# Second MoE layer by seven half-size products per 512-token block, with whole-batch q/k loads and 4-byte block transposes, in a fused attention and MoE kernel

## The chip, the cores and the metric

The kernel runs on one core of a Trainium2 chip. The metric is the device time of one execution in microseconds (us), on the slowest core, which here is the only core. A "ratio" below is the mean time of one kernel's fast runs over the mean of the other's fast runs of the same rounds, so it is not quite the ratio of the medians that are quoted beside it. Executions over 1.5% slower than the fastest of the same kernel are left out of the means.

Engines in the profile: PE is TensorE, PEld its weight loads, DVE is VectorE, ACT is ScalarE, POOL is GpSimd. L194 is line 194 of the kernel that the line comes from, so the numbers differ between kernels.

## The reference

Eight batches of eight heads, 576 tokens of 64 numbers each, are attended in chunks of 64 tokens. The result is laid out as x with 4608 tokens of 512 numbers, and passes through two matrix layers with a swish between them.

```python
# q, k, v: [8, 8, 576, 64];  w_in [512, 2048];  w_out [2048, 512];  beta [2048]
scores = scale * q_c @ k_c^T                # per chunk of 64 tokens
attn   = softmax(scores)
x      = (attn @ v_c).transpose(0, 2, 1, 3).reshape(4608, 512)
h      = x @ w_in
g      = h * (1 / (1 + exp(-beta * h)))
out    = g @ w_out                          # [4608, 512]
```

The kernels compute the sigmoid by a tanh: ScalarE makes `sg = tanh(beta/2 * h)`, VectorE makes `gt = (sg + 1) * h`, and the output is scaled by 0.5.

## The kernel before

Work is cut into blocks of 512 tokens (the first two of 256). For a block, sixteen groups `m` of four matmuls make the first layer. Each group fills one PSUM buffer `hps`; ScalarE reads it, then VectorE reads it and so frees it. The second layer makes four output tiles of sixteen matmuls each. Both layers share four PSUM buffers (pool `ps_p`).

```python
ps_p = tile_pool(name="ps_p", bufs=4, space=PSUM)

def emit_m(j, m):                           # first layer, one group
    hps = ps_p.tile([128, n], FP32, tag="p", name="hps")
    for kk in range(KDM):                   # 4 matmuls 128x512
        nc.tensor.matmul(out=hps, lhsT=w_in16[...], rhs=xt_t[j][:, kk, :], ...)
    nc.scalar.activation(out=sg, in_=hps, func=Tanh, scale=...)
    nc.vector.scalar_tensor_tensor(out=gt_t[j][:, m, :], in0=sg, scalar=1.0, in1=hps,
                                   op0=ALU.add, op1=ALU.mult)     # frees hps

def emit_t(j, t):                           # second layer, one tile of 128 tokens
    ops = ps_p.tile([128, DM], FP32, tag="p", name="ops")
    for kk in range(KFF):                   # 16 matmuls 128x512
        nc.tensor.matmul(out=ops, lhsT=gt_t[j][:, kk, ...], rhs=w_out16[:, kk, :], ...)
    nc.scalar.activation(out=osb, in_=ops, func=Copy, scale=0.5)  # frees ops

def emit_T(u):                              # q and k of 256 tokens; 2-byte elements,
    ...                                     # output step of 2 elements = 4 bytes
    nc.vector.transpose(out=t[:, :, :, :, r], in_=a[:, :, r, :]...)
# [...] loads, scores, values and the order of emission are cut here
```

In steady state the order is: groups m = 0 to 3 of block j, then the second layer of block j-1 with the attention of the next block between its tiles, then groups 4 to 15 of block j. VectorE's instructions appear in the traces in the order of emission: in the timeline after, below, an evacuation whose input is ready at 165.59 us starts at 171.06 us, behind four transposes that were emitted before it.

The softmax here doesn't subtract the row's maximum and nothing guards it: scores larger than these inputs give would overflow.

## Time and profile before

| | before |
|---|---|
| time, median of 4 runs | 347.41 us (346.66 to 349.46) |
| span of the profiled run | 348.3 us |
| TensorE busy | 288.9 us (83%) |
| VectorE busy | 175.7 us (50%) |
| start of the first first-layer matmul | 40.98 us |
| one block in steady state | 30.80 us |

The page of the kernel before: total busy times, then the busy share of TensorE in 40 slices (in tenths), then the share of each engine in the chain of work that ended last.

```profile
PE 288.9 (83%) x2944; PEld 142.9 (41%) x2944; DVE 175.7 (50%) x305; ACT 144.5 (41%) x234; POOL 77.2 (22%) x100
...
PE   0110274983998599999999999999999999999995
...
PE 77%; DMA 14%; DVE 3%; issue 2%; POOL 2%; ACT 1%; ACTq 0%; DVEq 0%; POOLq 0%
```

TensorE starves in the first third of the slices, which is a matter of loading (its longest wait, of 21.3 us, is for a transposed tile, while DMA is at nine tenths), and then is full to the end. The chain says the same: 77% of it is TensorE.

The chain of the kernel before, one block in steady state. Columns: start, duration, what.

```profile
200.69 13.81 PE hps L181 x64
214.87 3.56 PE ops L197 x16
219.44 3.56 PE ops L197 x16
223.37 3.56 PE ops L197 x16
227.93 3.56 PE ops L197 x16
231.49 13.81 PE hps L181 x64
```

One block lasts 231.49 - 200.69 = 30.80 us: 64 matmuls of each layer, 13.81 us for 64 (216 ns apart), and some 3 us of attention between the tiles. TensorE waits for nobody here, so a shorter second layer would shorten the block directly, if TensorE still waits for nobody afterwards.

Two neighbouring lines of its timeline, in the first layer. The bracket at the end of a line is the idle time of that engine before it, and what ended it.

```profile
205.04 0.69 ACT L189 ACTIVATE sg<-hps,beta_sb 128x512 f32<-128x512 f32 x1 [0.17 <-PE hps L181]
205.76 0.69 DVE L190 SCALAR_TENSOR_TENSOR gt<-sg,hps 128x512 f16<-128x512 f32 x1 [0.17 <-ACT sg L189]
```

VectorE spends 0.69 us of every 0.86 us on evacuations while the first layer runs. In that stretch it has 0.17 us to spare per group, although over the whole span it is busy only half the time.

### The profile page before, as it was taken

The numbers are of one execution on the slowest core, as the hardware profiler recorded it, in microseconds if no ns is written. First come the engines' busy times: TensorE is split into PE (matmuls) and PEld (weight loads), VectorE is DVE, ScalarE is ACT, GpSimd is POOL, SyncE is SP. The second block draws the span as 40 slices with busy tenths as digits, with TensorE's granted clock in tenths as the row PEclk, the third lists the DMA queues.
The fourth block names the chain that finished last, engine by engine and source line by source line (L and its number), as shares of the span: only waits on it lengthen the run. The fifth ranks groups of instructions, "written<-read, shape, count | busy, mean of one in ns | idle before, by whom it ended". The sixth has DMA issues, their size and how long they took to land.

```text
span 348.3 us, 7008 instructions
## 1 busy us (share of the span) xinstructions
PE 288.9 (83%) x2944; PEld 142.9 (41%) x2944; DVE 175.7 (50%) x305; ACT 144.5 (41%) x234; POOL 77.2 (22%) x100
## 2 busy tenths in 40 slices
PE   0110274983998599999999999999999999999995
PEld 0110263561443245445544444444444444444442
DVE  1413083662649264685377468637745822720700
ACT  1110153361357222752573275257427623732711
POOL 8628286803053035005402100000000000000000
PEclk9999997896799899999999999999999999999999
DMA  9999999999095949909952900420131042002011
GB/s 97 186 178 186 194 158 169 173 181 147 15 150 52 88 78 180 107 10 122 189 48 51 192 31 2 108 77 0 49 98 39 2 98 86 2 30 86 6 60 60
DMA packets 106223, 32.97 MB, mean 95 GB/s; under 512 B 97488, under 2 KB 101584, under 8 KB 106192
## 3 DMA queue, kind: packets, MB, share of 16 engines
q0 software_dynamic: 79360, 18.36, 61.9%
q1 hardware_dynamic: 26832, 14.17, 17.8%
q8 instruction: 23, 0.38, 0.5%
q14 instruction: 8, 0.07, 0.1%
HBM read 36.71 MB, written 9.44 MB: 132 GB/s over the span
## 4 chain that ended last, share of the span: by engine, by line
PE 77%; DMA 14%; DVE 3%; issue 2%; POOL 2%; ACT 1%; ACTq 0%; DVEq 0%; POOLq 0%
PE ops L197 37%; PE hps L181 34%; DMA ku<-in_k_dram 6%; PE x L156 3%; DMA xt_99<-x_362 2%; DMA xt_101<-x_865 2%; DMA xt_100<-x_548 2%; DMA xt_102<-x_1414 2%; DVE qT L122 1%; DVE kT L122 1%; DVE gt L190 1%; POOL qu L87 1%; POOL vbig L95 1%; ACT sg L189 0%; POOL ku L87 0%
## 5 line engine op out<-in xcount | busy, mean ns | idle before, releaser
L190 DVE SCALAR_TENSOR_TENSOR gt<-sg,hps 128x512 f16<-128x512 f32 (+1 forms) x160 | 100.5, 634 | 99.4 <-ACT sg L189 99.1
L189 ACT ACTIVATE sg<-hps,beta_sb 128x512 f32<-128x512 f32 (+1 forms) x160 | 102.4, 645 | 72.8 <-PE hps L181 68.1
L197 PE MATMUL ops<-w_out_97,gt 128*128 128x512 f16 x576 | 129.9, 380 | 0.0
L181 PEld LDWEIGHTS <-w_in_96 128*128 128x128 f16 x640 | 64.7, 102 | 107.0 <-issue 42.4
L197 PEld LDWEIGHTS <-gt 128*128 128x128 f16 x576 | 54.1, 98 | 62.9 <-issue 0.5
L205 ACT ACTIVATE osb<-ops 128x512 f32<-128x512 f32 x36 | 21.5, 597 | 109.9 <-PE ops L197 95.5
L87 POOL DMA_DIRECT2D qu<-in_q_dram x24 | 19.0, 795 | 98.9 <-DVE qT L122 55.7
L95 POOL DMA_DIRECT2D vbig<-in_v_dram x40 | 33.9, 862 | 8.3 <-DMA w_in_96<-in_moe_w_in_dram 5.2
L122 DVE STREAM_TRANSPOSE kT<-ku 128x512 f16<-128x512 f16 x36 | 24.2, 722 | 21.7 <-DMA ku<-in_k_dram 21.7
L181 PE MATMUL hps<-xt_99,w_in_96 128*128 128x256 f16 x64 | 10.0, 323 | 23.1 <-DMA xt_99<-x_362 21.3
L122 DVE STREAM_TRANSPOSE qT<-qu 128x512 f16<-128x512 f16 x36 | 23.4, 699 | 0.0
L162 DVE RECIPROCAL rd<-x 128x8 f32<-128x8 f32 x36 | 7.2, 199 | 32.1 <-PE x L156 32.1
L181 PE MATMUL hps<-xt_101,w_in_96 128*128 128x512 f16 x64 | 17.4, 431 | 5.9 <-issue 5.1
L137 PEld LDWEIGHTS <-kT 32*64 32x64 f16 x1152 | 11.5, 111 | 22.0 <-DVE kT L122 9.1
L87 POOL DMA_DIRECT2D ku<-in_k_dram x24 | 18.9, 789 | 5.8 <-DMA w_out_97<-in_moe_w_out_dram 4.5
L181 PE MATMUL hps<-xt_102,w_in_96 128*128 128x512 f16 x64 | 15.8, 411 | 3.9 <-DMA xt_102<-x_1414 3.9
L181 PE MATMUL hps<-xt_100,w_in_96 128*128 128x256 f16 x64 | 9.5, 309 | 6.2 <-DMA xt_100<-x_548 4.4
L181 PE MATMUL hps<-xt_103,w_in_96 128*128 128x512 f16 x64 | 14.1, 379 | 0.0
L181 PE MATMUL hps<-xt_104,w_in_96 128*128 128x512 f16 x64 | 14.1, 379 | 0.0
L181 PE MATMUL hps<-xt_105,w_in_96 128*128 128x512 f16 x64 | 14.1, 379 | 0.0
L181 PE MATMUL hps<-xt_106,w_in_96 128*128 128x512 f16 x64 | 14.1, 379 | 0.0
L181 PE MATMUL hps<-xt_107,w_in_96 128*128 128x512 f16 x64 | 14.1, 379 | 0.0
(190 smaller groups left out, 124.4 us busy)
## 6 DMA issues: line engine op xcount, KB each, us to landing
out_dram<-osb SPq DMA_DIRECT2D x36, 256.0 KB, 2.0
vbig<-in_v_dram POOLq DMA_DIRECT2D x32, 128.0 KB, 7.4
qu<-in_q_dram POOLq DMA_DIRECT2D x12, 256.0 KB, 6.6
ku<-in_k_dram POOLq DMA_DIRECT2D x12, 256.0 KB, 8.2
w_in_96<-in_moe_w_in_dram POOLq DMA_DIRECT2D x4, 512.0 KB, 12.2
w_out_97<-in_moe_w_out_dram POOLq DMA_DIRECT2D x4, 512.0 KB, 8.8
qu<-in_q_dram POOLq DMA_DIRECT2D x4, 192.0 KB, 4.1
ku<-in_k_dram POOLq DMA_DIRECT2D x4, 192.0 KB, 7.6
```

Source lines behind the costliest of these rows:

```text
L87: nc.gpsimd.dma_start(out=t[off // 2:(off + n) // 2], in_=src[b, :, s:s + n, :].rearrange("h (p r) d -> p h r d", r=2),)
L95: nc.gpsimd.dma_start(out=vbig[off:off + n, i, :, 0:D], in_=v[b, :, s:s + n, :].rearrange("h p d -> p h d"),)
L122: nc.vector.transpose(out=t[:, :, :, :, r], in_=a[:, :, r, :].rearrange("p h (e i) -> p h e i", e=2),)
L137: nc.tensor.matmul(out=sc[c // 2][o0:o0 + 64, h, :], lhsT=kt[p0:p0 + 32, h, e].rearrange("p i r -> p (i r)"), rhs=qt[p0:p0 + 32, h, e].rea ...
L156: nc.tensor.matmul(out=x[p0:p0 + 64, h // 4, h % 4, 0:D + 1], lhsT=et[p0:p0 + 64, h, :], rhs=vbig[p0:p0 + 64, i, h, 0:D + 1],)
L162: nc.vector.reciprocal(out=rd, in_=x[:, :, :, D:D + 1])
L181: nc.tensor.matmul(out=hps, lhsT=w_in16[:, kk, m * 128:(m + 1) * 128], rhs=xt_t[j][:, kk, :], start=(kk == 0), stop=(kk == KDM - 1),)
L189: nc.scalar.activation(out=sg, in_=hps, func=ACTF.Tanh, scale=beta2_sb[:, m:m + 1])
L190: nc.vector.scalar_tensor_tensor(out=gt_t[j][:, m, :], in0=sg, scalar=1.0, in1=hps, op0=ALU.add, op1=ALU.mult)
L197: nc.tensor.matmul(out=ops, lhsT=gt_t[j][:, kk, t * 128:(t + 1) * 128], rhs=w_out16[:, kk, :], start=(kk == 0), stop=(kk == KFF - 1),)
L205: nc.scalar.activation(out=osb, in_=ops, func=ACTF.Copy, scale=0.5)
```

## The change

The intent is to do less work on TensorE, the engine that bounds the kernel. For a 512-token block the second layer is a product of two matrices, each cut into 2x2 parts. Strassen's scheme (here in Winograd's form) makes it with seven products of half size instead of eight. Seven products are 112 matmuls of 128x256 where 64 of 128x512 were before. The scheme pays with additions: four sums of parts of `gt` for each block, four of `w_out` once, and sums of products at the end. At the same time q and k are loaded for a whole batch in runs of 18 tokens where it was 2, are transposed in blocks as 4-byte words, and the heads sit on four row quadrants of 32 partitions. Block 0 keeps a plain second layer; block 1's attention is emitted after it, with transposes on TensorE.

The diff, cut to its core:

```diff
 def emit_T:
-    nc.vector.transpose(out=t[:, :, :, :, r], in_=...)              # 128x512, 2-byte
+    nc.vector.transpose(                                            # 128x576, 4-byte
+        out=dst[b][:, h2]....bitcast(FP32).rearrange("p (t r) -> p r t", r=RUN),   # RUN = 18
+        in_=src[b][:, h2]....bitcast(FP32).rearrange("p (r d) -> p r d", r=RUN))
+
+def emit_sums(j, a, n):                      # VectorE, 4 ops of 128x1024 fp16
+    tt(out=s1[:, lo], in0=g[:, lo, dn], in1=g[:, hi, dn], op=ALU.add)
+    tt(out=s2[:, lo], in0=s1[:, lo], in1=g[:, lo, up], op=ALU.subtract)
+    tt(out=s3[:, lo], in0=g[:, lo, up], in1=g[:, lo, dn], op=ALU.subtract)
+    tt(out=s4[:, lo], in0=g[:, hi, up], in1=s2[:, lo], op=ALU.subtract)
+
+def steps_L2(j):                             # seven products of 16 matmuls 128x256
+    st0: A  = g11*b11;  ScalarE u1 = A/2     # four PSUM buffers: A, B, D, C
+    st1: B  = g12*b21;  VectorE out11 = B/2 + u1
+    st2: A += s2*t2;    ScalarE u2
+    st3: D  = g22*t4
+    st4: A += s3*t3;    ScalarE u3;  VectorE out21 = D/2 + u3;  GpSimd w1 = u2 - u3
+    st5: C  = s4*b22
+    st6: A += s1*t1;    ScalarE o22 = A/2;  GpSimd w2 = w1 + o22;  VectorE out12 = C/2 + w2
 [...]
 for j in range(1, NB):
     for m in range(KFF):
-        if m == 4: ... emit_t(j - 1, t) with attention steps between
+        if m == 4 and j >= 2:
+            for n, st in enumerate(steps_L2(j - 1)):
+                st()
+                if at and n < 6:
+                    at.pop(0)()              # one attention step
+            if j + 2 < B:
+                for h2 in range(2):
+                    emit_T(j + 2, h2)        # four transposes
         emit_m(j, m)
+        if m in (11, 15):
+            emit_sums(j, m - 11, 4)
```

The products `st0` to `st6` are written as formulas here; in the kernel each is sixteen matmul calls and the named operations.

## The prediction

> **What bounds it now.** The page's engine table has TensorE busy 83%. The chain of waits shows two phases. Up to about 85 us TensorE starves: the first first-layer matmul starts at 40.98 us, after a 21.3 us wait for a transposed tile, and DMA is at nine tenths in the slices. From 139 us TensorE never waits: successive 512-token blocks are 30.80 us apart (169.89, 200.69, 231.49): 64 first-layer and 64 second-layer 128x512 matmuls (13.81 us each, 216 ns apart) plus about 3.1 us of attention. In the first layer each 0.69 us VectorE evacuation is followed by 0.17 us idle.

> **Removed.** Strassen makes 112 matmuls of 256 columns out of 64 of 512 in the second layer. The timeline shows 256-column matmuls with a weight load each at a pace of 109 ns (20 in 2.35 us), so 12.2 us replaces 13.8: 1.6 us per block, for 8 of 9 blocks: 13 us. Eight transposes of 512 per block become about four of 576.

> **Added, on VectorE, which is in order.** Per block: eight fp16 sums of 128x1024. [...] Also three output combinations (0.69 us each, as the same op is today); the third waits for a ScalarE copy (0.60) and then a GpSimd add[...].

> **On the critical path.** Only four PSUM buffers serve both layers. An evacuation frees its buffer about 1.75 us after its matmuls; the other three cover 2.6 us, so slack is about 0.9 us. Four sums[...] come after m=11 and m=15: about 2 us of TensorE stall each, the second when product A wants a buffer. After product seven the third combination holds VectorE about 2 us waiting for GpSimd, [...]: another 3 us in blocks with transposes. Walking the instruction order with these durations, a block takes about 35.5 us (29.1 of TensorE work plus 6.5 stalled) where transposes are, 33.5 without, against 30.8 now. So the saved 1.6 us turns into a loss of 3 to 5 us per block.

> **Start.** PE transposes replace DMA transposes in blocks 0 and 1[...]. First layer of block 0 starts near 27 us (now 41); its plain second layer ends near 59; block 1's attention is then emitted serially, TensorE mostly idle about 18 us; block 1's first layer starts near 77. This gains about 11 us on the present start.

> **Sum:** 77 + 21 + 4x35.8 + 2x33.8 + 30 + 12.2 + 4: about 355; with cold-clock matmuls, 357 us. Range 343 to 372. Chances: faster by over 2% 0.10, within 2% 0.32, slower by over 2% 0.58.

> **What would show it.** Right: second-layer matmuls 109 ns apart; TensorE idle of about 2 us before product A and around m=8 and the next m=0, released by VectorE evacuations; VectorE busy over 65%; blocks 33 to 37 us apart; a TensorE hole of 15 to 20 us near 60 us. Wrong: block distance near 29.5 us (sums hidden), or first-layer starts before 20 us.

> **What would make it wrong.** [...] 4-byte block transposes at half rate: about +9 us. Sums much faster than thought, or the hole at 60 us small: below 343.

The sum came to 355 us, and to 357 with 2 us for the low clock. Where the text shows a cut there stood a duration, or a claim about packets, that no trace or run of this case had shown: what a sum, a GpSimd addition and a transpose cost, when the first batch lands, and a risk of slower sums. The terms of the waits were worked out with these durations. So the waits of 2 and 3 us, the blocks of 35.5 and 33.5 us (35.8 and 33.8 in the sum), the 9 us of the other risk and the share of VectorE are estimates that no trace had shown. The 1.75 us of an evacuation is an estimate too; in the trace before, 1.61 us lie between the start of a group's last matmul (201.39) and the end of its evacuation (203.00). "Cold-clock matmuls" are matmuls at a lower granted clock, which that trace has: the clock is 0.50 from 85.09 to 90.00 us, and 16 matmuls from 85.09 us on take 6.40 us, where 16 at 216 ns would be 3.5 us.

## The result

| | before | after |
|---|---|---|
| time, median of 4 runs | 347.41 us (346.66 to 349.46) | 376.0 us (375.01 to 376.22) |
| ratio, 95% interval | | 1.080 (1.076 to 1.084) |
| span of the profiled run | 348.3 us | 373.1 us |
| mean granted TensorE clock | 0.968 | 0.939 |

The changed kernel is correct and 8% slower. The prediction had 357 us, with a range up to 372; the direction was right and the size was not.

The same lines of the page after:

```profile
PE 290.0 (78%) x3296; PEld 173.5 (47%) x3296; DVE 220.1 (59%) x354; ACT 140.0 (38%) x216; POOL 83.8 (22%) x82
...
PE   0149995479589867995889588958899699889893
...
PE 48%; DVE 32%; issue 8%; ACT 4%; DMA 4%; POOL 3%; POOLq 0%; DVEq 0%
```

TensorE's slices no longer stay at nine. Its busy time did not fall at all, although it has less to compute; matmuls on a slowed clock count as longer (at a clock of 0.50, 5 or 6 of 128x512 begin in 1.70 us, at 1.00 it is 9; see the windows below). VectorE, which was 3% of the chain, is now 32% of it.

Who waits for whom, after. Columns: engine, what waits, for what; us in total, times, longest.

```profile
DVE osb L275 <- POOL w L314: 26.3, 8, 4.3
PE hps L194 <- DVE gt L205: 23.8, 10, 3.9
...
PE oA L257 <- DVE gt L205: 10.4, 8, 1.4
```

TensorE loses 34 us to evacuations by VectorE, where the first layer lost 4.4 us to them before. VectorE in turn waits 26 us for the last GpSimd addition of each block.

The next lines are one block of the timeline after, in the order of time. `osb<-oC,w` is the last combination of the second layer, the four STREAM_TRANSPOSE are q and k for two blocks ahead, `gt<-sg,hps` are the evacuations that free first-layer buffers, L219 to L222 are the sums.

```profile
164.81 1.27 POOL L314 TENSOR_TENSOR w<-w,o 128x512 f32<-128x512 f32 x1 [3.19 <-issue]
...
166.12 0.69 DVE L275 SCALAR_TENSOR_TENSOR osb<-oC,w 128x512 f32<-128x512 f32 x1 [2.98 <-POOL w L314]
...
166.73 1.25 DVE L118 STREAM_TRANSPOSE qT<-qu 128x576 f32<-128x576 f32 x1
...
167.82 1.24 DVE L118 STREAM_TRANSPOSE kT<-ku 128x576 f32<-128x576 f32 x1
...
168.90 1.23 DVE L118 STREAM_TRANSPOSE qT<-qu 128x576 f32<-128x576 f32 x1
169.98 1.24 DVE L118 STREAM_TRANSPOSE kT<-ku 128x576 f32<-128x576 f32 x1
171.06 2.46 DVE L205 SCALAR_TENSOR_TENSOR gt<-sg,hps 128x512 f16<-128x512 f32 x4
171.79 9.80 PE L194 MATMUL hps<-xt,w_in 128*128 128x512 f16 x32 [3.90 <-DVE gt L205]
...
179.69 0.69 DVE L219 TENSOR_TENSOR s<-gt 128x1024 f16<-128x1024 f16 x1
...
182.96 3.61 PE L194 MATMUL hps<-xt,w_in 128*128 128x512 f16 x16 [1.37 <-DVE gt L205]
...
188.00 1.91 PE L257 MATMUL oA<-w_out,gt 128*128 128x256 f16 x16 [1.43 <-DVE gt L205]
```

Read it as one story. VectorE stands idle for 2.98 us because its next instruction waits for GpSimd (whose addition takes 1.27 us of that and itself comes after TensorE's last product and a copy by ScalarE). Then it does four transposes, one every 1.08 us, together 4.3 us (166.73 to 171.06). Only then come the evacuations. Meanwhile TensorE has filled all four buffers and waits 3.90 us. The 32 matmuls after that wait take 9.80 us, although 32 at 216 ns would be 6.9 us. The other two waits of a block, before the first group of the next block (182.96) and before product A (188.00), are 1.4 us each; both come behind four sums in a row. In the two blocks without transposes VectorE's wait for GpSimd is there too, and TensorE then waits only 0.27 us: it takes the transposes behind that wait to make the long one.

Why the 32 matmuls were slow is seen in windows around the wait. Columns: window, its length, TensorE busy time with the number of matmuls, granted clock; the last two columns, for DMA, are not used here.

```profile
164.00:167.90 3.90, 3.61 (x16) 1.00 0.48 107
...
171.80:173.50 1.70, 1.70 (x5) 0.50 0.98 140
173.50:175.20 1.70, 1.70 (x6) 0.50 1.05 202
175.20:176.90 1.70, 1.70 (x6) 0.50 1.20 186
...
178.60:180.30 1.70, 1.70 (x9) 1.00 2.45 157
```

After the wait the clock is 0.50 for about 5 us. In windows of 0.1 us the clock goes to 0.50 between 2.6 and 4.1 us after TensorE's last matmul, in all four blocks. The way back took 2.7, 5.6, 3.6 and 2.7 us of matmuls. So the wait is paid twice, once as a wait and once as slow matmuls.

The last table of the profile after: the stretches from one block's first group to that of the next, for blocks 1 to 7, then the last block's up to near its end. Columns: window, length, busy time of PE, PEld, DVE, ACT and POOL with the number of instructions, granted clock, and two for DMA.

```profile
78.20:103.76 25.56, 19.95 (x257) 8.36 (x257) 21.42 (x34) 12.92 (x20) 5.07 (x6) 0.83 1.30 103
103.76:143.40 39.64, 33.59 (x368) 19.65 (x369) 26.53 (x40) 14.87 (x23) 7.58 (x8) 0.89 0.76 83
...
221.43:259.50 38.07, 30.96 (x368) 19.05 (x368) 24.88 (x40) 15.56 (x24) 2.53 (x2) 0.96 0.16 44
259.50:292.20 32.70, 29.50 (x368) 18.75 (x368) 20.64 (x36) 15.56 (x24) 2.54 (x2) 1.00 0.18 50
```

There are two kinds of block. Four blocks with transposes last 38.1 to 39.6 us; two without last 32.7 and 32.8 us at full clock. Both are longer than the 30.80 us of before. From one product A to the next the distances are 38.1, 39.5, 38.5 and 38.1 us with transposes and 32.7 us without. The excess of 5.4, 6.8, 5.8 and 5.4 us is accounted for in each block: a wait of 3.90 us, and 32 matmuls that took 8.39, 9.80, 8.75 and 8.37 us in place of 6.9.

### The profile page after: what moved, and what is told of

It is laid out like the page before. It is cut to its first block, busy times and chain, and to the rows that moved or that the text cites. A ratio compares the mean times of both kernels' runs of the same rounds, so it can differ in the third digit from the quotient of the medians.

```text
span 373.1 us, 7694 instructions
## 1 busy us (share of the span) xinstructions
PE 290.0 (78%) x3296; PEld 173.5 (47%) x3296; DVE 220.1 (59%) x354; ACT 140.0 (38%) x216; POOL 83.8 (22%) x82
## 4 chain that ended last, share of the span: by engine, by line
PE 48%; DVE 32%; issue 8%; ACT 4%; DMA 4%; POOL 3%; POOLq 0%; DVEq 0%
PE hps L194 17%; PE oA L257 13%; DVE gt L205 8%; PE oD L257 4%; PE oB L257 4%; DVE qT L118 4%; DMA vb<-in_v_dram 4%; DVE kT L118 3%; PE ops L323 3%; PE sc L137 3%; DVE s L219 3%; DVE x L167 3%; DVE s L220 3%; DVE s L222 2%; DVE s L221 2%
## 5 line engine op out<-in xcount | busy, mean ns | idle before, releaser
L194 PE MATMUL hps<-xt,w_in 128*128 128x512 f16 x576 | 144.6, 410 | 29.1 <-DVE gt L205 23.8
L202 ACT ACTIVATE sg<-hps,beta 128x512 f32<-128x512 f32 x144 | 99.0, 688 | 97.0 <-PE hps L194 55.9
L194 PEld LDWEIGHTS <-w_in 128*128 128x128 f16 x576 | 59.2, 104 | 108.8 <-issue 54.5
L205 DVE SCALAR_TENSOR_TENSOR gt<-sg,hps 128x512 f16<-128x512 f32 x144 | 93.0, 681 | 22.2 <-ACT sg L202 22.0
L257 PEld LDWEIGHTS <-s 128*128 128x128 f16 x512 | 48.1, 98 | 6.3
L257 PE MATMUL oA<-tw,s 128*128 128x256 f16 x384 | 46.0, 273 | 0.0
L146 ACT ACTIVATE et<-sc 128x512 f16<-128x512 f32 x36 | 19.5, 594 | 44.9 <-PE sc L137 44.4
L167 DVE TENSOR_TENSOR x<-x,rd 128x512 f16<-128x512 f32 x36 | 24.9, 691 | 1.2
L275 DVE SCALAR_TENSOR_TENSOR osb<-oD,u 128x512 f32<-128x512 f32 x8 | 5.5, 692 | 33.8 <-ACT u L268 33.8
L118 DVE STREAM_TRANSPOSE qT<-qu 128x576 f32<-128x576 f32 x16 | 19.9, 1241 | 9.4 <-DMA qu<-in_q_dram 9.4
L257 PE MATMUL oA<-w_out,gt 128*128 128x256 f16 x128 | 15.3, 272 | 10.4 <-DVE gt L205 10.4
L118 DVE STREAM_TRANSPOSE kT<-ku 128x576 f32<-128x576 f32 x16 | 19.8, 1236 | 0.8 <-DMA ku<-in_k_dram 0.8
```

The lines of the kernel that those rows point to most:

```text
L118: nc.vector.transpose(out=dst[b][:, h2].rearrange("p t r e -> p (t r e)").bitcast(FP32).rearrange("p (t r) -> p r t", r=RUN), in_=src[b][: ...
L146: nc.scalar.activation(out=et, in_=sc[s], func=ACTF.Exp, scale=scale)
L167: nc.vector.tensor_tensor(out=x16, in0=x[:, :, :, 0:D], in1=rd.to_broadcast([128, 2, 4, D]), op=ALU.mult,)
L194: nc.tensor.matmul(out=hps, lhsT=w[:, kk, m // 2, m % 2, :], rhs=xt_t[j][:, kk, :], start=(kk == 0), stop=(kk == KDM - 1),)
L202: nc.scalar.activation(out=sg, in_=hps, func=ACTF.Tanh, scale=beta2[:, m % 2, m // 2:m // 2 + 1])
L257: nc.tensor.matmul(out=bank[name][:, i, :], lhsT=a[:, kk, i * 128:(i + 1) * 128], rhs=b[:, kk, :], start=(first and i == 0 and kk == 0), s ...
```

## The experiments

The theory after reading the two traces: VectorE's *order* is what costs. Its extra work stands in front of evacuations, in places where only four buffers cover for it, and the largest piece (transposes behind a GpSimd wait) also drops the clock. There were three rivals. First, VectorE simply has too much work with Strassen's scheme, wherever it is put. Second, the second layer is innocent, and the loss comes from the other parts of the change (loads, transposes, the serial start). Third, the low clock is a state of the run and no consequence of the waits.

Twelve kernels were run. Each edit is against the changed kernel.
### The plain second layer in the changed kernel

```diff
 def steps_L2(j):
+    return [tile(t) for t in range(4)]       # 16 matmuls 128x512 each, ScalarE copy, store
-                        if at and n < 6:
-                            at.pop(0)()
+                        for _ in range((1, 2, 1, 2)[n]):
+                            if at: at.pop(0)()
-        emit_tw()
-                if m in (11, 15):
-                    emit_sums(j, m - 11, 4)
```

> Only the Strassen part is undone: blocks 1 to 8 get the plain second layer (64 matmuls of 512 columns), no sums, no combinations on VectorE, nothing on GpSimd but loads. Correct result. Theory A (VectorE's added work delays evacuations, and TensorE waits for PSUM buffers): TensorE has 1.6 us more work per block but 5 to 8 us fewer stalls, so 338 to 346 us, faster than the changed kernel's 376. Rival B (the loss sits in the new attention part: loads, transposes, row quadrants, serial start): it stays at 368 us or more, since Strassen itself saves 13 us of TensorE time.

Measured: 362.65 us (362.33 to 363.46), ratio 1.044 (1.037 to 1.050), correct. The expected time was missed, and by the experiment's own fault. Six attention steps on four tiles put two value products in a row, and the second waits for the single `x` buffer. From its waits:

```profile
PE x L159 <- DVE x L167: 13.1, 14, 1.0
...
PE hps L194 <- DMA xt<-x: 7.6, 1, 7.6
```

Of these 13 us the changed kernel has 3.3 and the kernel before has none; of the 7.6 us the changed kernel has 2.4. So the run says only that Strassen's part costs some 13 us (376.0 to 362.65) even against a plain layer with these waits; it was repeated with a better arrangement below.

### No sums (wrong)

```diff
-        s1, s2, s3, s4 = s_t[j]
+        s1, s2, s3, s4 = [g[:, 0:NM, 0:HT], g[:, NM:KFF, 0:HT], ...]   # parts of gt in their place
-                if m in (11, 15):
-                    emit_sums(j, m - 11, 4)
```

> The 8 fp16 sums per block are left out, and the products take slices of gt in their place (wrong result on purpose); matmul count, combinations and transposes stay. Theory A: two stalls of about 2 us per block go, about 351 us (346 to 356). Rival C (the loss comes from the 256-column products, the combinations or the wait for GpSimd, and the sums are hidden): 370 us or more.

Measured: 356.77 us (355.21 to 358.58), ratio 1.027 (1.021 to 1.034); wrong (relative error 1.6). Just above the expected range. Blocks without transposes fall to 29.6 us from 32.7; the difference of 3.1 us is about the two waits of 1.4 us. The waits at the transposes are unchanged: TensorE still waits 15.6 us in four pieces of 3.9. One wait before block 2 is longer here than in the changed kernel, 6.0 us against 2.4.

### No transposes after batch 2 (wrong)

```diff
 def emit_T(b, h2):
+    if b >= 3:
+        qT[b], kT[b] = qT[2], kT[2]
+        return
```

> The block transposes of batches 3 to 7 are left out, the scores take batch 2's tiles instead (wrong result on purpose). Theory A: the walls of four 1.09 us transposes before the evacuations go; block distance with transposes falls from 38.5 to about 33 us, in all about 356 us (352 to 361). Rival: transposes are hidden behind TensorE, no change (374 to 378).

Measured: 348.38 us (346.95 to 349.16), ratio 1.003 (0.997 to 1.008), the same as the kernel before. The comparison still called it correct: q and k are small, so the softmax is nearly uniform whatever they are. For this kernel a pass of the check says nothing about q and k. It saved 27.6 us, more than the 20 expected. Every block is now 32.7 us, the clock is 0.968 as before the change, and TensorE's longest wait for an evacuation is 1.4 us. Twenty transposes of 1.08 us are 22 us of VectorE time; taking them away saves more than they last, because the slowed clock goes with them.

### Four forms of the block transpose, measured side by side

```diff
 def emit_T(b, h2):
+    if b == 2: transpose(4-byte, contiguous output)         # L120
+    if b == 3: transpose(2-byte, contiguous output)         # L123
+    if b == 4: transpose(2-byte, output step 72 bytes)      # L126
     otherwise: transpose(4-byte, output step 72 bytes)      # L130, as in the change
```

> Measures block transposes in four forms on the same tiles (wrong result on purpose): batch 2: 4-byte, 576 elements, output contiguous; batch 3: 2-byte, 1152 elements, contiguous; batch 4: 2-byte, 1152 elements, strided output; batches 0, 1, 5, 6, 7 as in the change (4-byte, output step 72 bytes). If the strided output is what makes 576 elements cost 1.24 us, the contiguous 4-byte form drops[...]; if the 4-byte width itself is slow, it stays at 1.2 us.[...]

Measured: 393.79 us, one run; only the instruction times are used. Groups by form; the last figure before the bar is the mean of one in ns.

```profile
L130 DVE STREAM_TRANSPOSE kT<-ku 128x576 f32<-128x576 f32 x10 | 12.4, 1239 | 0.9 <-DMA ku<-in_k_dram 0.9
...
L126 DVE STREAM_TRANSPOSE kT<-ku 128x1152 f16<-128x1152 f16 x2 | 10.8, 5394 | 0.0
...
L123 DVE STREAM_TRANSPOSE kT<-ku 128x1152 f16<-128x1152 f16 x2 | 2.7, 1332 | 0.0
...
L120 DVE STREAM_TRANSPOSE kT<-ku 128x576 f32<-128x576 f32 x2 | 1.5, 734 | 0.0
```

The 4-byte width is not what makes the transpose slow: with a contiguous output, 576 words take 734 ns, little more than half the time of the 2-byte form (1332 ns). The output step of 18 words, which follows from the runs of 18 tokens, takes 1239 ns. At the step of 72 bytes the 2-byte form takes 5.39 us, four times the 1.33 us of its contiguous output.

### The plain second layer, one attention step between half tiles

```diff
 def steps_L2(j):
+    return [half(n) for n in range(8)]       # tile n//2, matmuls 8*(n%2) to 8*(n%2)+7
-        emit_tw()
-                if m in (11, 15):
-                    emit_sums(j, m - 11, 4)
```

> As the first plain run, but the six attention steps stand apart, one after each half of a plain tile, so that no two value products follow each other (in the first plain run TensorE waited 13 us for the x buffer, which the change does not do). Theory A: about 350 us (347 to 353), so that Strassen as written costs 24 to 28 us net. Rival B (the rest of the change is what costs): stays at 360 us or more.

Measured: 338.59 us (338.43 to 338.91), ratio 0.972 (0.971 to 0.974), correct. This is better than expected: blocks are 30.54 us apart, and the four transposes, at the same place and with the same duration, cost nothing. Without the combination that waits for GpSimd, VectorE gets at them earlier: in one block they begin 2.5 us before the second layer ends (156.39 and 158.88 us), while TensorE still has work. So the rest of the change is worth 2.8% over the kernel before, and Strassen's part, as written, costs the 10.7 points between the ratios 1.080 and 0.972, about 37 us. The second rival falls. Taken with the run without transposes, this says that the long waits need both: the transposes, and a second layer whose last combination holds them back.

### Runs of two tokens from batch 2 on

```diff
 def load_qk(b):
+    if b >= 2: ... "(c t r) d -> t c (r d)", t=32, r=2       # runs of two tokens
 def emit_T:
+    if b >= 2: out "p (c t r) -> p c r t", t=32, r=2         # output step 8 bytes
```

> Batches 2 to 7 load q and k in runs of two tokens, so that the 4-byte block transposes write with a step of 8 bytes instead of 72; correct result, all else as in the change (more and smaller loads on GpSimd's queue). If the output step is what costs, a transpose takes 0.75 us instead of 1.24, the wall after the second layer falls from 4.3 to about 2.6 us, the 3.9 us wait of TensorE to about 2.2 us, and the clock no longer falls to half after it: 354 to 360 us. If the clock's fall is not tied to the wait's length, only 11 us are saved: 363 to 367 us. If the 4-byte width costs: no change.

Measured: 367.79 us (362.94 to 368.56), ratio 1.049 (1.041 to 1.057), correct. One of the four runs (368.56 us) counts as slow and is not in the ratio. The transposes take 0.75 us as hoped (754 ns for q's, where the contiguous form took 751), and the wait falls from 3.90 to 2.2 us, but the time misses the expected 354 to 360. Two of its four waits, with the matmuls that follow, then two windows of 2 us, of those matmuls:

```profile
135.71 1.67 PE L213 MATMUL hps<-xt,w_in 128*128 128x512 f16 x7 [2.22 <-DVE gt L224]
...
170.80 8.75 PE L213 MATMUL hps<-xt,w_in 128*128 128x512 f16 x32 [2.21 <-DVE gt L224]
```

```profile
137.70:139.70 2.00, 2.00 (x11) 1.00 1.48 142
...
172.80:174.80 2.00, 2.00 (x7) 0.50 1.39 133
```

Two waits of equal length; after one the clock stays at 1.00, after the other it is 0.50. The block distances show it in two of the four blocks with transposes: 34.9, 36.8, 35.1 and 36.8 us. So a wait of 2.2 us can also cost the clock, and does so or not from case to case. That the clock would hold was the author's guess; the changed kernel had it at 1.00 through its waits of 1.4 us and at 0.50 after those of 3.90 us. In windows of 0.1 us the changes of the clock to and from 0.50 lie at 171.5, 174.9, 243.2 and 246.6 us; in the packed trace, which keeps each of them, they are 1, 20 and 1 steps of 3.413 us apart, and the 13 distances between those of the changed kernel are whole numbers of such steps too, from 1 to 35. TensorE's busy time between points of this grid, for the first two of the four waits (columns as before):

```profile
133.97:137.39 3.42, 1.69 (x8) 1.00 1.37 166
168.11:171.52 3.41, 1.20 (x7) 1.00 1.22 170
```

A wait of 6.0 us for one transposed tile, up to 107.93 us, is part of the miss as well; in the changed kernel it is 2.4 us.

### The sums later, as four whole ones in the second layer

```diff
-                if m in (11, 15):
-                    emit_sums(j, m - 11, 4)
 def steps_L2(j):
+    emit_sums(j, 0)                          # s1, s2: 128x2048, before st0
 def st2():  + emit_sums(j, 1)                # s3
 def st3():  + emit_sums(j, 2)                # s4
```

> The same sums, in four operations of 128x2048 instead of eight of 128x1024, emitted inside the second layer's stretch, where VectorE has idle time, instead of after m=11 and m=15. Correct result. Theory A (the sums cost only because they stand in front of evacuations): the waits before the next m=0 and before product A go, 354 to 360 us, as much as leaving the sums out (356.8). Rival (VectorE's total work is the limit): within 3 us of 376.

Measured: 356.69 us (356.14 to 356.98), ratio 1.024 (1.022 to 1.026), correct. This equals the kernel without sums (1.027). All the sums are done, each 1.22 us long, in a stretch where VectorE idled, and in steady blocks they cost nothing there (in the last two second layers, which have no attention between the products, TensorE waits 0.4 and 0.6 us for one). Blocks without transposes are 29.6 us.

### Block 1's attention inside block 0's second layer

```diff
         emit_m(0, m)
+        if m in (10, 13): emit_T(1, (m - 10) // 3)
-    emit_L2_plain(0); emit_tw(); emit_T(1, ...); emit_sc(2); emit_pv(4, True); ... emit_pv(7, True)
+    emit_L2_plain(0, [sc(2), pv(4), pv(5), sc(3), pv(6), pv(7)])   # one step per two kk; DMA transposes
```

> Block 1's attention is emitted inside block 0's plain second layer instead of after it (with DMA transposes instead of PE transposes). Correct result. Expected: the TensorE hole from 60 to 78 us closes to 1 to 4 us; 359 to 364 us. If loads are what holds block 1 back, the hole only moves: 370 us or more.

Measured: 378.77 us (376.85 to 379.62), ratio 1.087 (1.083 to 1.091), correct. The hole only moved; the second of the two outcomes came true. TensorE's longest wait after the first layer has begun:

```profile
78.95 5.12 PE L194 MATMUL hps<-xt,w_in 128*128 128x512 f16 x16 [10.87 <-DMA xt<-x]
```

The DMA transpose that it waits for took 13.27 us, while batch 3's loads were under way (65.54 to 78.81 us); the median on the page after is 2.3 us. That the loads were the cause was not tested.

### The same instructions, the four transposes one place earlier

```diff
                         st()
                         if at and n < 6: at.pop(0)()
+                        if n in (3, 5) and j + 2 < B:
+                            emit_T(j + 2, (3, 5).index(n))
                     if j + 2 < B:
-                        for h2 in range(2):
-                            emit_T(j + 2, h2)
```

> The change with one thing moved: the four block transposes of a steady block are emitted in two pairs after the fourth and the sixth step of the second layer, in front of the combination that waits for GpSimd, instead of behind it. Same instructions, correct result. If the order is what costs (theory A), the 3.9 us wait before m=8 and the half clock after it go in the four blocks with transposes: 355 to 361 us. If VectorE's total work in the block is the limit: within 3 us of 376.

Measured: 352.78 us (350.67 to 354.49), ratio 1.014 (1.008 to 1.020), correct; against the kernel before the verdict at 2% is unclear, against the ratio 1.080 of the change it is not. Nothing was removed and no instruction got faster; 23 us went away by order alone. Its timeline at the same point of a block:

```profile
158.73 1.25 DVE L118 STREAM_TRANSPOSE qT<-qu 128x576 f32<-128x576 f32 x1
...
159.82 1.24 DVE L118 STREAM_TRANSPOSE kT<-ku 128x576 f32<-128x576 f32 x1
...
161.79 0.69 DVE L275 SCALAR_TENSOR_TENSOR osb<-oC,w 128x512 f32<-128x512 f32 x1 [0.74 <-POOL w L314]
...
162.54 7.93 PE L194 MATMUL hps<-xt,w_in 128*128 128x512 f16 x36 [0.27 <-DVE osb L275]
```

The first pair of transposes (151.84 us) now runs inside the second layer, and the second pair, shown above, lies in the time in which VectorE would wait for GpSimd (0.74 us of idling are left of 2.98). TensorE waits 0.27 us in place of 3.90, and 36 matmuls take 7.93 us, so the clock is full. All blocks are 32.7 us, those with transposes too. The third rival falls: without the long wait the low clock is gone from all these blocks.

### Both: sums later and transposes earlier

Two edits are taken together: the sums of "The sums later" and the transposes of the section above.

> Sums inside the second layer's stretch and transposes in front of the last combination, together; the same VectorE work as in the change but for fewer, longer sums. Correct result. Theory A: blocks about 30 us apart, with or without transposes; 331 to 338 us. If VectorE's work (about 15 us of the 15.3 us stretch) overflows there: 345 us or more.

Measured: 332.92 us (331.6 to 333.95), ratio 0.958 (0.953 to 0.964), correct, inside the expected range. Its page, and its TensorE in one block:

```profile
PE 277.5 (84%) x3296; PEld 171.3 (52%) x3296; DVE 221.2 (67%) x322; ACT 139.9 (42%) x216; POOL 83.7 (25%) x82
```

```profile
157.26 11.38 PE L194 MATMUL hps<-xt,w_in 128*128 128x512 f16 x52 [0.27 <-DVE osb L279]
...
168.48 1.91 PE L261 MATMUL oA<-w_out,gt 128*128 128x256 f16 x16
```

VectorE does as much as in the changed kernel (221.2 us against 220.1), and the kernel is 43 us faster. Blocks are 29.6 us apart. From the last combination to product A TensorE does not wait once in a steady block. (Elsewhere one wait of 7.0 us for a transposed tile remains.) The first rival falls: with the same amount of VectorE work the loss is gone, so it was not the amount that made the changed kernel slow.

### Block 1's attention overlapped, with and without Strassen

These two ask what is left once the hole near 60 us is filled as well. Both put block 1's attention between half tiles of block 0's second layer, and block 2's into block 1's first layer, by transposes on TensorE that are emitted one step late. The first keeps Strassen as in the last section, with product D before the second A and s4 one product later. The second has the plain half tiles.

```diff
 both:
+            if m in (12, 15): emit_T(1, (m - 12) // 3)
-        emit_L2_plain(0); emit_tw(); ... emit_pv(7, True)
+        emit_L2_plain(0, [lambda: None] + in_parts(1))     # one step per half tile
+            at = in_parts(2) if j == 1 else attn(j + 1)
 first only:
-        return [st0, st1, st2, st3, st4, st5, st6]
+        return [st0, st1, st3, st2, st4, st5, st6]
 second only:
+    steps_L2 returns half tiles; no sums, no emit_tw
```

> As the last, and block 1's attention inside block 0's plain second layer, taken tile by tile so that PSUM buffers stay for PE transposes (emitted one step late), block 2's likewise by PE transposes; product D before A's second. Correct result. Product A of block 1 should start near 86 us instead of 110; 302 to 315 us, faster than both kernels.

> The same start with the plain second layer in all blocks. Correct result. From the half-tile plain run (30.54 us a block): 309 to 320 us. Its distance to the Strassen version shows what Strassen is worth once nothing waits: an estimated 8 to 12 us.

Measured, with Strassen: 319.44 us (319.24 to 322.92), ratio 0.921 (0.914 to 0.927). Plain: 321.75 us (320.33 to 324.02), ratio 0.926 (0.919 to 0.932). Both are correct and both beat the kernel before. Both missed their expected ranges: the first by 4 us, the second by 2. In the first, product A of block 1 starts at 96.35 us where 86 was expected. (Its profile is of the slowest of four runs, 322.92 us where the others have 319.2 to 319.5.) TensorE waits only 1.1 us for the values of batch 1, which landed late. The larger part is block 1's first layer, 29.9 us from 66.46 us on: VectorE is busy for 24.1 us of it, with four transposes, tile copies and evacuations at once, and the mean clock is 0.89. How the loss divides among these was not tested. Its blocks are 30.4 to 30.7 us with transposes, as product C now waits for the sum s4 (3.7 us in four times), and 29.8 without. The difference between the two kernels is half a point of ratio, and the intervals overlap. That Strassen is worth anything in this last arrangement was not shown. The expected 8 to 12 us are not there.

## Why the prediction was right or wrong

Right, by the trace after:

- The direction and the mechanism. Extra VectorE work stands in front of evacuations, four buffers cover for too little of it, and TensorE waits at the three predicted places: before the next block's first group, before product A, and near m = 8.
- Durations of the added operations that the trace before already showed: combinations 0.69 us (predicted 0.69), the seven products at 109 ns per matmul (109). The sums take 0.69 us and the GpSimd additions 1.27; what the prediction had for these rested on no trace. The idling before the third combination was put at about 2 us and is 3.0.
- The start: the first layer of block 0 at 29.3 us (27), that of block 1 at 78.2 (77), a TensorE hole from 60 to 78 us (15 to 20 us).

Wrong is the size of one term of the sum. The prediction put four transposes before the next evacuation, wrote "another 3 us in blocks with transposes", and in its sum made it 2 us per block (35.8 against 33.8). The sum, term by term, in us:

| term | predicted | measured, profiled run |
|---|---|---|
| up to the first layer of block 1 | 77 | 78.2 |
| from there to block 2 | 21 | 25.6 |
| four blocks with transposes | 143.2 | 155.7 |
| two blocks without | 67.6 | 65.5 |
| last block and end | 46.2 | 48.1 |
| cold clock, as a lump | 2 | inside the terms |
| sum | 357 | 373.1 |

Of the 16 us, 12.5 are in the four blocks with transposes. Two things were missed there. The transpose was taken to be about as short as the 0.70 to 0.72 us that the kernel before shows for another output layout; in the changed kernel one follows another every 1.08 us, and four take 4.3 us. The prediction named slow 4-byte transposes as a risk of 9 us, with the wrong reason (the width); the four forms show that it is the output step (734 ns contiguous, 1239 ns at 72 bytes). And with the longer run of transposes the wait grew to 3.90 us, after which TensorE ran part of the next 32 matmuls at half clock, which cost 1.5 to 2.9 us more per block. The prediction let TensorE wait and then go on at full speed, with a lump of 2 us for the clock in the whole kernel. The measured effect of the transposes is 5.4 to 6.8 us per block in place of 2.

The term of block 1 is 4.6 us too long for related reasons, which the trace shows and no experiment tests alone: four transposes (78.06 to 82.39) stand before its first evacuation, the mean clock there is 0.83, and a transposed tile is waited for 2.4 us. The blocks without transposes are 1 us shorter than predicted, because the waits behind the sums are 1.4 us and not 2. "VectorE busy over 65%" was wrong too: it is 59%. It was a poor witness, since the reordered kernel is at 67% and fast.

Behind these sizes stands the wider error, which experiments showed and the prediction did not consider: it took 3 us of loss per block as what Strassen costs here. In the reordered kernel the sums and combinations make TensorE wait only for the 0.27 us per steady block that is seen above. What remains of Strassen's own gain is smaller than computed: 29.6 us per block against 30.54 for the plain half tiles, 0.9 us of the predicted 1.6. Where the rest goes was not tested.

## What to carry to other kernels

VectorE started its instructions in the order of emission here (an evacuation whose input was ready at 165.59 us started at 171.06), so ask of every instruction added to it what stands behind it: work in front of the instruction that frees a buffer was paid by the engine that needs the buffer (3.90 us of TensorE's time behind four transposes), while the same work in an idle stretch, or ahead of an instruction that waits for another engine, cost next to nothing (the kernel became 43 us faster with the same busy time). Keep TensorE's waits short, since one of 3.9 us cost another 1.5 to 2.9 us of slow clock, and one of 2.2 us cost 1.7 us where it fell whole into one 3.413 us step of the clock's grid. Cost an instruction from a trace only if its access pattern is the same: the output step alone took a block transpose from 0.75 to 1.24 us.
